# Raw weights of layer 1's first steps in four buffers, their mask on VectorE, and loads in another order

## The chip, the cores and the metric

One core of one Trainium2 chip runs the whole program. The metric is device microseconds of an execution, the median of several runs. TensorE (PE) does the matmuls, VectorE (DVE), ScalarE (ACT) and GpSimd (POOL) the elementwise work, and SyncE (SP) issues every DMA, in the order in which the program lists them. Each engine works through its own instructions in order; the engines wait for one another by semaphores.

## The reference

Three layers follow one another: random-feature attention over 32 heads (4 batches of 8, here 16 pairs of heads), and two feed-forward layers over 2304 tokens.

```python
def phi(x):                                   # q and k scaled by D**-0.25
    proj = np.einsum('bhsd,md->bhsm', x, omega)
    h = proj - np.sum(x * x, axis=-1, keepdims=True) / 2.0
    h = h - np.max(h, axis=-1, keepdims=True)
    return np.exp(h) / np.sqrt(m)
kv = np.einsum('bhsm,bhsd->bhmd', k_p, v)
num = np.einsum('bhsm,bhmd->bhsd', q_p, kv)
den = np.einsum('bhsm,bhm->bhs', q_p, np.sum(k_p, axis=2))[..., None] + 1e-06
x = num / den                                 # to (2304, 512)
h = x @ w_in;  x = (h - np.tanh(h)) @ w_out                      # layer 1
h = x @ w_in2; x = (h / (1.0 + np.exp(-1.702 * h))) @ w_out2     # layer 2
```

All is float32. The weights are 512 x 2048 and 2048 x 512.

## The kernel before, in words

**Attention** runs in 16 periods, k = 0 to 15, one per pair of heads (`period`, L420). A period multiplies q and k with omega (`att_a`, L106, and `att_b`, L134), sums keys with values (`att_c`, L161), multiplies the previous pair's queries with that (`att_d`, L178), and transposes the pair before (`att_e`, L202), whose result ScalarE rounds (`att_e_hi`, L216) and VectorE subtracts from (`att_e_lo`, L221). PSUM has four tiles `hs` and one each of `y0` to `y3`. `att_c` writes `y0`, which `att_a` also wrote and ScalarE copies out first (L113); `att_e` and `att_d` both write `y2` and `y3`. The last period has no `att_b`. What is left of attention after it (`tail0` to `tail2`) is put between the first three matmul steps of layer 1.

**The layers** run in two phases of eight weight slices each, over blocks of tokens in the orders of `ORDER` (L36): four blocks of 512 tokens and one of 256, whose number is 4. A step (the loop at L550, index `si`) takes one slice of one block of 512: h = x times w_in, 12 matmuls (`h_mm`, L299), and, three steps later, y += g times w_out, another 12 (`y_mm`, L346 in layer 1, L350 in layer 2). A block of 512 has eight steps, the block of 256 has four with two slices each. h(n) and y(n) below are those of step n. Twelve are needed because each float32 operand is split in two parts, hi and lo, and three of the four products are taken. The third of the twelve is the first to read a weight's lo part.

Between h and y stands `elem1` (L316) in layer 1: ScalarE takes the square s (L319), a second square (L320) and tanh (L321), rounds the previous step's result (`ghi`, L311) and writes the mask m (L323); VectorE does L324 and L326, POOL the product L325, then VectorE's copy_predicated (L327) takes the second branch where the mask is set. POOL subtracts `ghi` from the result (`glo`, L313), a step later and ahead of its product.

**Weights** come as raw 64-bit words and are rebuilt in `conv_mid` (L531): ScalarE's `conv1` (L247, L249) and VectorE's `conv2a` and `conv2b` (L253, L258) in one step, ScalarE's `conv3` (hi, L268) and POOL's `conv4` (lo, L272) a step later, behind the next half slice's `conv1` on ScalarE. A half slice is one unit, in the order of `US` (L41). Eight units are converted during attention. Units 8 to 15 are converted in steps 1 to 8, one each; h(4) to h(7) read units 8 to 11 and y(4) to y(7) read units 12 to 15. A raw unit lies in one of two buffers `raw`; its load (`load_w`, L234) is issued when `conv4` has freed the buffer of the unit two before.

**x blocks** lie in two buffers `xb`. The next block is loaded in four parts, one per step (L584 to L590); phases that begin with the block that the one before ended with share its buffer.

Of the kernel before, what the change touches and what calls it, by code (L numbers as in the profile page):

```python
# [11 lines left out]
I32 = mybir.dt.int32  # L12
I64 = mybir.dt.int64
U16 = mybir.dt.uint16
AF = mybir.ActivationFunctionType
ALU = mybir.AluOpType
# [7 lines left out]
FP = NF // 2  # L24
# [4 lines left out]
THR2 = 0.25 ** 2  # L29
# [10 lines left out]
NATT = 8  # L40
# [4 lines left out]
def body(ctx, tc, qT, kT, v, om, w1, w2, out):  # L45
    nc = tc.nc
    DRAM = bass.MemoryType.DRAM

    def pool(name, c=ctx, **k):
        return c.enter_context(tc.tile_pool(name=name, bufs=1, **k))  # L50
# [3 lines left out]
    cv = pool("conv")  # L54
# [5 lines left out]
    ap = pool("attn", early)  # L60
# [9 lines left out]
    tb = cp.tile([128, 1], F32, name="tb")  # L70
# [4 lines left out]
    def pt(tag):  # L75
        return ps.tile([128, 512], F32, tag=tag, name=tag, bufs=4 if tag == "hs" else 1)
# [4 lines left out]
    N16 = B * NP  # L81
# [6 lines left out]
    def load_k(i):  # L88
        if i < N16:
            kin[i] = ap.tile([128, S], F32, tag="kt", name="kt", bufs=2)  # L90
            nc.sync.dma_start(out=kin[i], in_=kT[i // NP, i % NP])
# [64 lines left out]
    def att_c(i):  # L156
        kp, vt = kps.pop(i), vin.pop(i)
        c = pt("y0")
        for j in range(2):
            for st in range(ST):  # L160
                nc.tensor.matmul(  # L161
                    c[:, j * DV:j * DV + DV], kp[:, j, st, :], vt[:, j, st, :], start=(st == 0), stop=(st == ST - 1))
        return c
# [66 lines left out]
    raws = {}  # L230
# [3 lines left out]
    def load_w(ci):  # L234
        if ci >= NU:
            return
        u = US[ci]
        i, part = divmod(u, 2)
        src = (w1, w2)[i // NF]
        raws[u] = cv.tile([128, 512, 2], I32, tag="raw", name="raw", bufs=2)  # L240
        nc.sync.dma_start(
            out=raws[u], in_=src[i % NF, :, part, :].bitcast(I32).rearrange("p (a b) -> p a b", b=2))


    def conv1(u):
        c = raws[u][:, :, 1].bitcast(F32)
        nc.scalar.activation(out=c, in_=c, func=AF.Copy, scale=2.0 ** -112)  # L247
        top = raws[u].bitcast(U16).rearrange("p a (b h) -> p a b h", h=2)[:, :, 0, 1]
        nc.scalar.activation(out=raws[u][:, :, 0], in_=top, func=AF.Copy, scale=0.9998 * 2.0 ** -13, bias=-0.4995)  # L249
# [27 lines left out]
    xblk = {}  # L277

    def new_x(key):
        xblk[key] = xp.tile([128, 2, ND, 512], F32R, tag="xb", name="xb", bufs=2)  # L280

    def load_x(key, part):
        src = (xs, ys)[key[0]]
        t0, n = BLOCKS[key[2]]
        if part == 0:
            new_x(key)
        hl, c = divmod(2 * part, ND)
        nc.sync.dma_start(
            out=xblk[key][:, hl, c:c + 2, :n].bitcast(F32),
            in_=src[hl, c:c + 2, :, t0:t0 + n].rearrange("c p t -> p c t"))  # L290
# [14 lines left out]
    def gtile(tag, bufs, dt=F32):  # L305
        return gp.tile([128, 512], dt, tag=tag, name=tag, bufs=bufs)
# [6 lines left out]
        nc.gpsimd.tensor_tensor(out=lo, in0=g, in1=hi.bitcast(F32), op=ALU.subtract)  # L313
        parts += [hi, lo]

    def elem1(h, us):  # L316
        s, t, w = gtile("s", 2), gtile("t", 2), gtile("wq", 2)
        m = gtile("m", 1, mybir.dt.bfloat16)
        nc.scalar.activation(out=s, in_=h, func=AF.Square)  # L319
        nc.scalar.activation(out=w, in_=s, func=AF.Square, scale=QS, bias=qb)  # L320
        nc.scalar.activation(out=t, in_=h, func=AF.Tanh)  # L321
        split_prev()
        nc.scalar.activation(out=m, in_=s, func=AF.Relu, bias=tb)  # L323
        nc.vector.scalar_tensor_tensor(out=w, in0=w, scalar=QC, in1=h, op0=ALU.add, op1=ALU.mult)  # L324
        nc.gpsimd.tensor_tensor(out=w, in0=w, in1=s, op=ALU.mult)  # L325
        nc.vector.tensor_tensor(out=t, in0=h, in1=t, op=ALU.subtract)  # L326
        nc.vector.copy_predicated(out=w, mask=m.bitcast(mybir.dt.uint16), data=t)  # L327
        conv_mid(us)
        return w

    def elem2(h, us):
        s = gtile("wq", 2)
        nc.scalar.activation(out=s, in_=h, func=AF.Sigmoid, scale=1.702)  # L333
        nc.vector.tensor_tensor(out=s, in0=h, in1=s, op=ALU.mult)  # L334
        split_prev()
        conv_mid(us)
        return s
# [56 lines left out]
        nc.sync.dma_start(out=ys[1, d, :, t0:t0 + n], in_=ye)  # L394


    oms = ap.tile([128, M], F32, name="oms")
    nc.sync.dma_start(out=oms, in_=om)
    load_k(0)
    load_q(0)  # L400
    load_k(1)
    load_v(0)
# [6 lines left out]
    def warm_up(n, tag):  # L409
        w = pt(tag)  # L410
        for i in range(n):
            nc.tensor.matmul(w, warm[:, :128], warm, start=True, stop=True)
# [4 lines left out]
    ci = [0]  # L417
    cprev, clast = [], []

    def period(k):  # L420
        old, new, last = cprev[:], [], clast[:]
        if 1 < k < 14 and k % 3:
            new.append(ci[0])
            ci[0] += 1
        cprev[:] = new
        clast[:] = old
        if k > 1:
            att_d_norm(k - 2, 1)
        if k > 0:
            att_sub(k - 1, 1)  # L430
            att_exp(k - 1, 1)
        for x in last:
            conv4(US[x], nc.vector)
        for x in old:
            conv2a(US[x])
        a = att_a(k)
        load_q(k + 2)
        if k + 1 < N16:
            tiles, mx = att_b(k + 1)
            load_k(k + 3)  # L440
        att_a_copy(k, a)
        if k == 0:
            make_identity(nc, ident)
            warm_up(1, "y3")
        if k > 1:
            parts = att_e_parts(k - 2, att_e(k - 2))
            att_e_hi(parts)
        if k + 1 < N16:
            for t in range(4):
                att_b_max(tiles, mx, t)  # L450
            for t in range(4):
                att_b_exp(k + 1, tiles, mx, t)
        if k > 1:
            att_e_lo(k - 2, parts)
        c = att_c(k)
        load_v(k + 2)
        att_c_copy(k, c)
        for x in old:
            conv2b(US[x])
        att_sub(k, 0)  # L460
        att_exp(k, 0)
        for x in old:
            conv3(US[x])
        if k == 1:
            load_w(0)
            load_w(1)
        for x in new:
            conv1(US[x])
        if k > 0:
            att_d(k - 1)  # L470
            att_d_norm(k - 1, 0)
        for x in last:
            load_w(x + 2)

    warm_up(2, "y0")
    tiles, mx = att_b(0)
# [5 lines left out]
    for k in range(N16):  # L482
        period(k)
# [20 lines left out]
    tails = [tail0, tail1, tail2]  # L504


    pend = deque()
    wnext = []
    steps = []
    seq = []  # L510
# [20 lines left out]
    def conv_mid(xs):  # L531
        for x in xs:
            conv1(US[x])
        for x in cprev:
            conv3(US[x])
            conv4(US[x], nc.gpsimd)
        for x in xs:
            conv2a(US[x])
            conv2b(US[x])
        wnext.extend(x + 2 for x in cprev)  # L540
        cprev[:] = xs

    def split_prev():
# [4 lines left out]
    gprev = []  # L548
    per = len(steps) // 4
    for si, (key, k, fs) in enumerate(steps):  # L550
        if si == len(tails):
            early.close()
            late["p"] = pool("late")
        moe, ph, bi = key
        n = BLOCKS[bi][1]
        ii = [moe * NF + f for f in fs]
        pos = seq.index(key)
        first, last = k == 0, fs[-1] == ph * FP + FP - 1
        h = h_mm(key, [wt[i] for i in ii], n)
        if si < len(tails):  # L560
            tails[si]()
        P, sp = divmod(si, per)
        us = []
        if P == 0 and sp <= 2 * FP - NATT:
            room = NATT - 2 * FP + sp
        else:
            room = min(2 * FP, max(0, (sp - (9 if P == 0 else 4)) * 2 * FP // 26))
        if ci[0] < 2 * FP * (P + 1) + room and conv_ok(ci[0]):
            us.append(ci[0])
            ci[0] += 1  # L570
        if first:
            y = [pt(f"y{d}") for d in range(ND if moe == 0 else n // 128)]
        ev = do_y() if len(pend) == LAG else None
        if ev:
            evac(*ev, 0)
        g = (elem2 if moe else elem1)(h, us)
        if ev:
            evac(*ev, 1)
        else:
            evac_split()  # L580
        gg = []
        gprev.append((g, gg))
        pend.append((key, y, ii, gg, first, last))
        xk = k - (1 if n == 512 else 0)  # L584
        if 0 <= xk < 4 and pos + 1 < len(seq):
            new = seq[pos + 1]
            if (new[0], new[2]) == (moe, bi):
                xblk[new] = xblk[key]
            else:
                load_x(new, xk)  # L590
        if ph and k >= FP // (512 // n) - 2:
            for d in range(2):
                load_part(moe, bi, d + 2 * (last))
        while wnext:
            load_w(wnext.pop(0))
    split(gprev.pop())
    while pend:
        ev = do_y()
# [43 lines left out]
```

## Time and profile before

| | us |
|---|---|
| median of 3 runs (942.77 to 944.05) | 943.16 |
| the profiled execution | 942.97 |
| its span | 941.2 |
| PE busy in it | 921.3 |
| DVE, ACT, POOL busy | 478.5, 515.7, 447.0 |

The span runs from the first to the last instruction; the execution's own time is 1.8 us more. TensorE is busy 98% of it, the other engines about half. A busy share of TensorE is not its speed: the profile also gives the clock that it was granted, in the mean 0.998 of the full one.

### The profile page before, as it was taken

The numbers are of one execution on the slowest core, as the hardware profiler recorded it, in microseconds if no ns is written. First come the engines' busy times: TensorE is split into PE (matmuls) and PEld (weight loads), VectorE is DVE, ScalarE is ACT, GpSimd is POOL, SyncE is SP. The second block draws the span as 40 slices with busy tenths as digits, with TensorE's granted clock in tenths as the row PEclk, the third lists the DMA queues.
The fourth block names the chain that finished last, engine by engine and source line by source line (L and its number), as shares of the span: only waits on it lengthen the run. The fifth ranks groups of instructions, "written<-read, shape, count | busy, mean of one in ns | idle before, by whom it ended". The sixth has DMA issues, their size and how long they took to land.

```text
span 941.2 us, 13426 instructions
## 1 busy us (share of the span) xinstructions
PE 921.3 (98%) x4918; PEld 775.5 (82%) x4918; DVE 478.5 (51%) x709; ACT 515.7 (55%) x1041; POOL 447.0 (47%) x330
## 2 busy tenths in 40 slices
PE   8999998899999999999999999999999999999998
PEld 6888886678888898888887888888888888888887
DVE  5999977566666653767767523432341212121212
ACT  6888867667768765777787624443442211211211
POOL 3555546555665653668686734433433222222221
PEclk9999999999999999999999999999999999999999
DMA  6777634252514243345464632425411233140302
GB/s 193 232 253 240 222 120 152 75 179 89 179 57 146 74 143 120 120 149 184 152 206 151 205 111 100 146 91 179 157 64 49 69 111 128 51 157 12 123 1 90
DMA packets 59890, 124.24 MB, mean 132 GB/s; under 512 B 6704, under 2 KB 11952, under 8 KB 59824
## 3 DMA queue, kind: packets, MB, share of 16 engines
q1 hardware_dynamic: 59824, 123.38, 39.5%
q8 instruction: 39, 0.64, 0.3%
q14 instruction: 27, 0.22, 0.1%
HBM read 90.32 MB, written 33.03 MB: 131 GB/s over the span
## 4 chain that ended last, share of the span: by engine, by line
PE 78%; POOL 6%; DVE 4%; ACT 4%; DMA 3%; issue 3%; SPq 1%; POOLq 0%; ACTq 0%; DVEq 0%
PE hs L299 34%; PE y L350 21%; PE y L346 14%; PE y L178 3%; PE y L161 3%; POOL wq L325 2%; DMA xb<-xs 2%; POOL glo L313 2%; POOL w L272 2%; PE y L106 1%; PE hs L134 1%; DVE wq L327 1%; DVE pq L120 1%; DMA raw<-w 1%; PE y L202 1%
## 5 line engine op out<-in xcount | busy, mean ns | idle before, releaser
L299 PE MATMUL hs<-xb,w 128*128 128x512 f32 (+1 forms) x1920 | 420.9, 369 | 5.8 <-POOL w L272 2.8
L299 PEld LDWEIGHTS hs<-xb,w 128*128 128x128 f32 x1920 | 335.3, 189 | 70.1 <-POOL w L272 4.5
L313 POOL TENSOR_TENSOR glo<-wq,ghi 128x512 fp32r<-128x512 f32 x144 | 192.2, 1335 | 392.2 <-ACT ghi L311 392.2
L346 PE MATMUL y<-ghi,w 128*128 128x512 f32 (+1 forms) x640 | 194.1, 371 | 4.2 <-ACT w L268 2.4
L333 ACT ACTIVATE wq<-hs 128x512 f32<-128x512 f32 x72 | 43.0, 597 | 271.9 <-PE hs L299 270.4
L350 PE MATMUL y<-w,ghi 128*128 128x512 f32 x576 | 188.6, 389 | 0.0
L334 DVE TENSOR_TENSOR wq<-hs,wq 128x512 f32<-128x512 f32 x72 | 49.6, 690 | 237.9 <-ACT wq L333 237.9
L327 DVE COPY_PREDICATED wq<-m,t 128x512 f32<-128x512 uint16 x72 | 99.3, 1379 | 117.2 <-POOL wq L325 115.1
L346 PEld LDWEIGHTS y<-ghi,w 128*128 128x128 f32 x640 | 116.9, 189 | 26.2 <-ACT w L268 2.9
L350 PEld LDWEIGHTS y<-w,ghi 128*128 128x128 f32 x576 | 108.2, 188 | 22.4
L346 PE MATMUL y<-glo,w 128*128 128x512 f32 (+1 forms) x320 | 118.2, 369 | 0.0
L350 PE MATMUL y<-w,glo 128*128 128x512 f32 x288 | 112.1, 389 | 0.0
L311 ACT CAST ghi<-wq 128x512 fp32r<-128x512 f32 x144 | 88.1, 612 | 25.7 <-DVE wq L327 24.9
L325 POOL TENSOR_TENSOR wq<-wq,s 128x512 f32<-128x512 f32 x72 | 93.1, 1292 | 15.1 <-DVE wq L324 15.1
L116 POOL PARTITION_ALL_REDUCE mq<-pq x32 | 64.4, 2059 | 63.7 <-ACT pq L114 60.0
L272 POOL TENSOR_TENSOR w<-raw,w 128x512 fp32r<-128x512 f32 x56 | 74.0, 1321 | 11.3 <-ACT w L268 11.3
L319 ACT ACTIVATE s<-hs 128x512 f32<-128x512 f32 x72 | 42.9, 596 | 64.5 <-PE hs L299 64.4
L346 PEld LDWEIGHTS y<-glo,w 128*128 128x128 f32 x320 | 60.6, 190 | 10.0
L350 PEld LDWEIGHTS y<-w,glo 128*128 128x128 f32 x288 | 54.1, 188 | 10.8
L258 DVE SCALAR_TENSOR_TENSOR raw<-raw 128x512 int32<-128x512 int32 x64 | 61.2, 957 | 1.9
L324 DVE SCALAR_TENSOR_TENSOR wq<-wq,hs 128x512 f32<-128x512 f32 x72 | 49.0, 680 | 18.6 <-ACT t L321 18.5
L320 ACT ACTIVATE wq<-s,qb 128x512 f32<-128x512 f32 x72 | 52.2, 725 | 6.6
(63 smaller groups left out, 927.7 us busy)
## 6 DMA issues: line engine op xcount, KB each, us to landing
raw<-w SPq DMA_DIRECT2D x64, 512.0 KB, 3.8
xb<-xs SPq DMA_DIRECT2D x28, 512.0 KB, 4.8
xb<-ys SPq DMA_DIRECT2D x28, 512.0 KB, 4.8
vt<-v SPq DMA_DIRECT2D x16, 325.0 KB, 3.3
kt<-kT SPq DMA_DIRECT2D x16, 288.0 KB, 3.2
qt<-qT SPq DMA_DIRECT2D x16, 288.0 KB, 3.1
op<-ye SPq DMA_DIRECT2D x18, 256.0 KB, 2.1
ye<-op SPq DMA_DIRECT2D x18, 256.0 KB, 6.1
```

The lines of the kernel that those rows point to most:

```text
L116: nc.gpsimd.partition_all_reduce(mqs[i, j], pq[:, j, :], channels=128, reduce_op=bass.bass_isa.ReduceOp.max)
L258: nc.vector.scalar_tensor_tensor(out=c, in0=c, scalar=3, in1=z, op0=ALU.logical_shift_left, op1=ALU.bitwise_or)
L272: eng.tensor_tensor(out=wt[i][:, part, 1, :], in0=raws.pop(u)[:, :, 1].bitcast(F32), in1=wt[i][:, part, 0, :].bitcast(F32), op=ALU.subtract)
L299: nc.tensor.matmul(h[:, j * n:j * n + n], w[:, 0, a, kt * 128:kt * 128 + 128], x[:, c, kt, :n], start=(k == 0), stop=(k == 11))
L311: nc.scalar.copy(out=hi, in_=g)
L313: nc.gpsimd.tensor_tensor(out=lo, in0=g, in1=hi.bitcast(F32), op=ALU.subtract)
L320: nc.scalar.activation(out=w, in_=s, func=AF.Square, scale=QS, bias=qb)
L325: nc.gpsimd.tensor_tensor(out=w, in0=w, in1=s, op=ALU.mult)
L327: nc.vector.copy_predicated(out=w, mask=m.bitcast(mybir.dt.uint16), data=t)
L334: nc.vector.tensor_tensor(out=s, in0=h, in1=s, op=ALU.mult)
L346: nc.tensor.matmul(y[d][:, :n], w[:, 1, a, d * 128:d * 128 + 128], g[c][:, j * n:j * n + n], **fl)
L350: nc.tensor.matmul(y[d], g[c][:, c0:c0 + 128], w[:, 1, a, :], **fl)
```

## The change

Units 8 to 15 get a tag of their own, `rw`, with four buffers in attention's pool, whose space is given back at step 9 instead of step 3. The first four of them are loaded in periods 12 to 15, the other four as `conv4` frees a buffer; `load_next` says what is loaded when a unit is done. Units 16 and 17 take the two `raw` buffers during attention. In steps 0 to 8 the mask is a comparison on VectorE (a tensor_scalar of s) instead of a Relu on ScalarE. A block's x may be loaded a block earlier where the phase in between shares its buffer, and in the block of 256 two parts per step, from its first step. The first key load is issued ahead of omega's; the zero matmul of period 0 is left out; in period 15 `att_c` stands ahead of `att_e`.

```diff
@@ load_w
-        raws[u] = cv.tile([128, 512, 2], I32, tag="raw", name="raw", bufs=2)
+        if NATT <= ci < 2 * FP:
+            raws[u] = ap.tile([128, 512, 2], I32, tag="rw", name="rw", bufs=4)
+        else:
+            raws[u] = cv.tile([128, 512, 2], I32, tag="raw", name="raw", bufs=2)
...
+    def load_next(ci):
+        if NATT <= ci < 2 * FP:
+            if ci + 4 < 2 * FP:
+                load_w(ci + 4)
+        else:
+            load_w(ci + 2 if ci >= 2 * FP or ci + 2 < NATT else ci + 2 + 2 * FP - NATT)
@@ elem1
-        nc.scalar.activation(out=m, in_=s, func=AF.Relu, bias=tb)
+        if si > 2 * FP - NATT:
+            nc.scalar.activation(out=m, in_=s, func=AF.Relu, bias=tb)
+        else:
+            nc.vector.tensor_scalar(out=m, in0=s, scalar1=THR2, scalar2=None, op0=ALU.is_gt)
@@ first loads
+    load_k(0)
     oms = ap.tile([128, M], F32, name="oms")
     nc.sync.dma_start(out=oms, in_=om)
-    load_k(0)
@@ period
             make_identity(nc, ident)
-            warm_up(1, "y3")
+        if k + 1 == N16:
+            c = att_c(k)
         if k > 1:
             parts = att_e_parts(k - 2, att_e(k - 2))
...
-        c = att_c(k)
+        if k + 1 < N16:
+            c = att_c(k)
...
         for x in last:
-            load_w(x + 2)
+            load_next(x)
+        if k > 11:
+            load_w(NATT + k - 12)
@@ conv_mid
-        wnext.extend(x + 2 for x in cprev)
+        wnext.extend(cprev)
@@ the steps
-        if si == len(tails):
+        if si == 2 * FP - NATT + 1:
             early.close()
...
-        xk = k - (1 if n == 512 else 0)
-        if 0 <= xk < 4 and pos + 1 < len(seq):
-            new = seq[pos + 1]
+        for new in seq[pos + 1:pos + 3]:
             if (new[0], new[2]) == (moe, bi):
                 xblk[new] = xblk[key]
-            else:
-                load_x(new, xk)
+                continue
+            if k == 0:
+                xnext[key] = deque(range(4)) if new not in xblk else deque()
+            for j in range(2 if n == 256 else 1):
+                if xnext[key] and (k > 0 or n == 256):
+                    load_x(new, xnext[key].popleft())
+            break
...
         while wnext:
-            load_w(wnext.pop(0))
+            load_next(wnext.pop(0))
```

In the orders below a row is line, operation, tile written <- tiles read, columns, and how many in a row. First TensorE's order in period 15 and up to h(1), before:

```order
L106 MATMUL y_1730<-qt,omd 128x64
L106 MATMUL hs<-qt,omd 128x64
L202 MATMUL y_1745<-ident,xt 128x128 x4
L202 MATMUL y_1746<-ident,xt 128x128
L161 MATMUL y_1760<-vt,kp 128x65 x10
L178 MATMUL y_1775<-kvz,pq 128x65 x6
L178 MATMUL y_1782<-kvz,pq 128x65 x4
L299 MATMUL hs<-xb,w 128x512 x12
L202 MATMUL y_1813<-ident,xt 128x128 x4
L202 MATMUL y_1814<-ident,xt 128x128
L299 MATMUL hs<-xb,w 128x512 x12
L178 MATMUL y_1857<-kvz,pq 128x65 x6
```

and after:

```order
L106 MATMUL y_1734<-qt,omd 128x64
L106 MATMUL hs<-qt,omd 128x64
L161 MATMUL y_1749<-vt,kp 128x65 x10
L202 MATMUL y_1760<-ident,xt 128x128 x4
L202 MATMUL y_1761<-ident,xt 128x128
L178 MATMUL y_1779<-kvz,pq 128x65 x6
L178 MATMUL y_1786<-kvz,pq 128x65 x4
L309 MATMUL hs<-xb,w 128x512 x12
L202 MATMUL y_1819<-ident,xt 128x128 x4
L202 MATMUL y_1820<-ident,xt 128x128
L309 MATMUL hs<-xb,w 128x512 x12
L178 MATMUL y_1863<-kvz,pq 128x65 x6
```

The ten matmuls of `att_c` (kp times vt) have moved ahead of the five transposes (ident and xt); `att_d` (kvz and pq) follows the transposes.

VectorE's order from the copy_predicated of one step to that of the next, between steps 3 and 4, before:

```order
L327 COPY_PREDICATED wq<-m,t 128x512
L253 SCALAR_TENSOR_TENSOR raw<-raw 128x512
L258 SCALAR_TENSOR_TENSOR raw<-raw 128x512
L324 SCALAR_TENSOR_TENSOR wq<-wq,hs 128x512
L326 TENSOR_TENSOR t<-hs,t 128x512
L327 COPY_PREDICATED wq<-m,t 128x512
```

and after:

```order
L340 COPY_PREDICATED wq<-m,t 128x512
L263 SCALAR_TENSOR_TENSOR rw<-rw 128x512
L268 SCALAR_TENSOR_TENSOR rw<-rw 128x512
L336 TENSOR_SCALAR m<-s 128x512
L337 SCALAR_TENSOR_TENSOR wq<-wq,hs 128x512
L339 TENSOR_TENSOR t<-hs,t 128x512
L340 COPY_PREDICATED wq<-m,t 128x512
```

The mask (m<-s) now stands between the second bit operation of the weight (rw or raw) and the first operation of the next step.

SP's order from the short block of phase 0 to that of phase 1 in layer 1 (raw are weights, xb parts of x, yp and ye partial y), before:

```order
L241 DMA raw<-w 128x1024 x4
L380 DMA yp<-ye 128x512 x4
L241 DMA raw<-w 128x1024
L288 DMA xb<-xs 128x2x512
L241 DMA raw<-w 128x1024
L288 DMA xb<-xs 128x2x512
L380 DMA yp<-ye 128x256 x4
L288 DMA xb<-xs 128x2x512
L362 DMA ye<-yp 128x256 x2
L288 DMA xb<-xs 128x2x512
L362 DMA ye<-yp 128x256 x2
```

and after:

```order
L244 DMA raw<-w 128x1024 x2
L298 DMA xb<-xs 128x2x512 x2
L244 DMA raw<-w 128x1024
L298 DMA xb<-xs 128x2x512 x2
L244 DMA raw<-w 128x1024
L393 DMA yp<-ye 128x512 x4
L244 DMA raw<-w 128x1024 x2
L393 DMA yp<-ye 128x256 x4
L375 DMA ye<-yp 128x256 x4
```

The four loads of x have moved ahead of the stores of the block before, and no load of x stands any more among the loads and stores of the short block's partial y.

## Rows read from the trace of the kernel before

**Rows 1.** TensorE's timeline, steps 4 to 9: start, us, what, [idle before]

```profile
148.54 2.60 PE L299 MATMUL hs<-xb,w 128*128 128x512 f32 x10 [0.84 <-POOL w L272]
...
174.30 0.50 PE L346 MATMUL y<-ghi,w 128*128 128x512 f32 x1 [2.42 <-ACT w L268]
...
175.68 0.74 PE L346 MATMUL y<-ghi,w 128*128 128x512 f32 x2 [0.65 <-POOL w L272]
...
189.00 0.74 PE L346 MATMUL y<-ghi,w 128*128 128x512 f32 x2 [0.51 <-POOL w L272]
```

**Rows 2.** List of waits: who for whom, us in all, times, longest

```profile
ACT raw L247 <- DMA raw<-w: 10.6, 6, 2.2
```

**Rows 3.** POOL's timeline in step 5: the weight subtraction

```profile
161.02 1.30 POOL L272 TENSOR_TENSOR w<-raw,w 128x512 fp32r<-128x512 f32 x1 [1.76 <-ACT w L268]
```

**Rows 4.** From the chain that ended last: start, us, what

```profile
175.68 3.97 PE y L346 x10
...
191.60 2.72 PE hs L299 x12
```

**Rows 5.** A stretch: busy us by engine, granted clock, DMA share, GB/s

```profile
178.00:180.00 2.00, 2.00 (x6) 1.51 (x6) 0.76 (x1) 0.70 (x2) 1.14 (x1) 0.52 0.25 98
```

**Rows 6.** TensorE's timeline at the two borders

```profile
356.87 2.15 PE L299 MATMUL hs<-xb,w 128*128 128x512 f32 x7
...
361.49 0.28 PE L346 MATMUL y<-ghi,w 128*128 128x256 f32 x1
...
643.82 1.75 PE L299 MATMUL hs<-xb,w 128*128 128x512 f32 x7
...
647.75 0.39 PE L350 MATMUL y<-w,ghi 128*128 128x512 f32 x1
```

**Rows 7.** Timelines of period 15 and tail0, TensorE and VectorE

```profile
123.38 0.77 PE L202 MATMUL y<-ident,xt 128*128 128x128 f32 x5
...
125.36 2.45 PE L161 MATMUL y<-vt,kp 128*128 128x65 f32 x20 [1.21 <-ACT pq L113]
...
127.64 2.40 PE L178 MATMUL y<-kvz,pq 128*128 128x65 f32 x20
...
132.66 0.71 PE L202 MATMUL y<-ident,xt 128*128 128x128 f32 x5
...
133.96 0.82 DVE L221 TENSOR_TENSOR xl<-y,xh 128x512 fp32r<-128x512 f32 x2 [2.39 <-ACT xh L216]
```

**Rows 8.** Groups by line: shapes, count, busy us, mean ns, idle before

```profile
L406 DVE TENSOR_SCALAR omd<-oms 128x128 f32<-128x128 f32 x1 | 0.2, 227 | 1.1 <-DMA oms<-om 1.1
...
L324 DVE SCALAR_TENSOR_TENSOR wq<-wq,hs 128x512 f32<-128x512 f32 x72 | 49.0, 680 | 18.6 <-ACT t L321 18.5
...
L190 DVE TENSOR_SCALAR rc<-y 128x6 f32<-128x6 f32 (+1 forms) x32 | 5.0, 155 | 0.0
```

**Rows 9.** Timelines of POOL and VectorE around 440 us

```profile
440.67 1.76 POOL L392 TENSOR_TENSOR ye<-ye,yh 128x512 fp32r<-128x512 f32 x1
...
439.47 1.85 DVE L327 COPY_PREDICATED wq<-m,t 128x512 f32<-128x512 uint16 x1 [1.25 <-POOL wq L325]
...
441.22 1.77 DVE L253 SCALAR_TENSOR_TENSOR raw<-raw 128x512 int32<-128x512 int32 x1
```

**Rows 10.** Timelines of VectorE and POOL in one undisturbed conversion step

```profile
479.52 1.84 DVE L327 COPY_PREDICATED wq<-m,t 128x512 f32<-128x512 uint16 x1 [2.50 <-POOL wq L325]
...
481.96 0.69 DVE L258 SCALAR_TENSOR_TENSOR raw<-raw 128x512 int32<-128x512 int32 x1
...
482.09 1.72 POOL L313 TENSOR_TENSOR glo<-wq,ghi 128x512 fp32r<-128x512 f32 x1 [1.35 <-ACT ghi L311]
...
485.09 1.84 DVE L327 COPY_PREDICATED wq<-m,t 128x512 f32<-128x512 uint16 x1 [1.24 <-POOL wq L325]
```

**Rows 11.** TensorE's timeline in period 1

```profile
14.20 0.69 PE L106 MATMUL y<-qt,omd 64*128 64x512 f32 x1 [0.63 <-ACT kvz L167]
```

**Rows 12.** DMA issues: KB each, median us to landing

```profile
raw<-w SPq DMA_DIRECT2D x64, 512.0 KB, 3.8
```

More of the change, by code (lines that the diff above doesn't have):

```diff
@@ L314, in split, with elem1 @@
         parts += [hi, lo]
-    def elem1(h, us):
+    def elem1(si, h, us):
         s, t, w = gtile("s", 2), gtile("t", 2), gtile("wq", 2)
@@ L507, in body @@
     pend = deque()
+    xnext = {}
     wnext = []
@@ L575, in body @@
             evac(*ev, 0)
-        g = (elem2 if moe else elem1)(h, us)
+        g = elem2(h, us) if moe else elem1(si, h, us)
         if ev:
```

## The prediction

> **What bounds the kernel now.** TensorE is busy nearly all the time, so I looked first for the places where it stands still, in the timeline of TensorE and in the list of waits; elsewhere it is fed without a gap and nothing that the change does can matter. There are two kinds of place.
>
> The first is layer 1's opening steps. In [rows 1] four of TensorE's waits stand with what ended them: the reader is to see that POOL's or ScalarE's write of a split weight releases TensorE, and that the third matmul of h(4) starts at 148.54 and that of y(4) at 175.68 us. Between them lie four steps of 6.79 us on average, where a step's 24 matmuls take 2 x 2.72 = 5.44 us [rows 4]. Why is the weight late? ScalarE waits for the raw weights six times, 10.6 us in all [rows 2]: a load starts when POOL's second half of an older weight has freed one of two buffers, and ScalarE cannot write the newer weight's first half before it, since that stands behind the waiting conversion. So POOL waits for ScalarE in turn (1.76 us at 161.02, [rows 3]), and load, conversion and subtraction form a ring that turns slower than TensorE. At 178 to 180 us the granted clock is 0.52, the 1.2 GHz level [rows 5], after TensorE had waited 2.42 and 0.65 us [rows 1]; ten matmuls then take 3.97 us where twelve take 2.72 at full clock [rows 4].
>
> The second kind is the block borders behind the 256-token block. [rows 6] shows h of the new block starting at 356.87 and the next y at 361.49: 4.62 us for work of 2.72, 1.90 lost. The other: 643.82 to 647.75, 1.21 lost. Both wait for the last part of x, issued in the short block's last step.
>
> **Borders: 3.1 us gained.** The parts of x are now issued a block earlier (first border) or two per step (second), at least two steps before they are needed, where they came in the step before. I take the whole 1.90 + 1.21 = 3.1 us. What could take it back is SP's order: loads of x now stand behind one raw load that waits for POOL, and the stores of partial y behind them; there are two steps for that. If the cover fails the gain is 0.
>
> **Order in the last attention period: 2.0 us lost.** Before, the transposes of head pair 13 run at 123.38, in the time in which TensorE waits 1.21 us for att_c's PSUM tile, and att_c follows at 125.36, att_d(14) at 127.64 [rows 7]. Att_c still waits for the same ScalarE copy; so it starts at 125.36 again, now with the gap empty, and the transposes come behind it, at 125.36 + (127.64 - 125.36) = 127.6. Att_d(14) writes the two PSUM tiles that the transposes wrote, so it also waits for ScalarE and VectorE to read them. How long that takes the next such pair shows: transposes at 132.66, VectorE's subtraction from 133.96, of which the first and larger of two takes 0.68 (as L324 does, [rows 8]): 1.98 us. Att_d(14) so starts at 129.6, 1.96 late, and TensorE runs from there to h(3) without waiting, so all that follows is late too. The bounds are 0 (if it is caught up behind) and 2.1 (both subtractions).
>
> **The mask on VectorE: 1.1 us more per step.** First its own time. A 128-column tensor_scalar takes 0.227 us (L406), a 512-column operation 0.680 (L324), a 6-column one 0.155 (L190) [rows 8]. The last two give 1.04 ns per column; at that pace 128 columns would take 0.28, so L406 runs at about half of it, and the mask takes 0.155 + 506 x 0.52 ns = 0.42 us. Bounds 0.23 and 0.68.
>
> Then where it stands. In VectorE's order it comes right behind the second bit operation of the weight conversion and ahead of the step's own L324. [rows 9] shows what can happen there: POOL's operation waits from 440.67 for VectorE's copy_predicated to end, and VectorE's next operation, L253, though ready, then takes 1.77 us, where L258, of the same kind, takes 0.69 undisturbed [rows 10]: the two engines exclude each other, and a waiting POOL goes ahead of VectorE's next. VectorE's operations with a PSUM operand (L324, [rows 8]) keep 0.68. Now one undisturbed conversion step [rows 10]: copy_predicated ends at 481.36 and, a step later, at 486.93, so a step takes 5.57 us; L258 begins at 481.96; POOL's L313 asks at 482.09, inside it, and ends at 483.81; then POOL's product, its weight subtraction and the next copy_predicated follow each other. The mask would stand behind L258 with L313 waiting: it starts at 483.81, takes 0.42, L324 0.68, and POOL's product starts at 484.9 instead of 483.8. The step becomes 5.57 + 1.1 = 6.67 us. This takes the mask for an operation that excludes POOL. Its operands are both in SBUF, as those of L253, L258 and L327 are, and none in PSUM, so those are the nearest rows; but they read two tensors and it reads one, so the other end (no exclusion, 5.57) stays as a rival.
>
> The Trainium skill speaks against the change here: "SBUF — State Buffer", section "Who interferes with whom", says that a tensor_scalar whose source and destination are in SBUF can run in a two-port mode, and that such an operation and a GpSimd instruction fully block each other; no row here shows it for that operation. By that page the step is the 6.67 us of the sum, without it 5.57.
>
> **Four raw buffers: the ring is gone, and the step of 6.67 takes its place.** The first eight weights' waits on DMA vanish; in their place stands the chain above. With h(4)'s third matmul at 148.54 + 1.96 + 1.1 = 151.6, y(4)'s comes four steps on, at 178.3, y(5)'s at 185.0, y(6)'s at 191.6. Step 9 has its mask on ScalarE again: y(7)'s at 197.2. Before, y(6) waits until 189.00 [rows 1], and y(7)'s third matmul comes 24 matmuls later, at 194.4. So steps 0 to 9 lose 2.8 us in all, the 1.96 among them. Between steps TensorE will wait over a microsecond each time, so a fallen clock is covered there, as is the relief of ScalarE, which had time to wait for DMA.
>
> **With one answer, nothing each.** The zero matmul in period 0: TensorE waits for ScalarE's kvz copy at 14.20 [rows 11] in any case, so its time is hidden. The key load ahead of omega: the first matmuls stand behind the two zero matmuls that remain. Four loads more in periods 12 to 15: a raw load takes 3.8 us to land [rows 12], no key or query load is left behind them that is needed sooner than one period later; one that came late would cost at most that.
>
> **Sum.** +2.8 - 3.1 = -0.3 us. Against the profiled execution (942.97 us, span 941.2) that is 942.7; against the median of the three runs, 943.16, it is 942.9, which I predict. A measurement tells about 0.2%, 1.9 us, from no change.
>
> **Rivals.**
> - The mask meets no POOL, or it is not held: the step stays 5.57, y(7) comes at 148.54 + 1.96 + 7 x 5.57 = 189.5, 4.9 early; with the borders 943.16 - 8.0 = 935.2. For it: a single source. Against: the pace of L406 looks like two columns at a time. 0.14.
> - The mask goes ahead of the waiting POOL: only its 0.42 is added, 6.0 a step; y(7) at 150.9 + 6 x 6.0 + 5.57 = 192.5, -1.9 - 3.1 = -5.0: 938.2. Against: rows 9. 0.08.
> - The late transposes cost nothing (slack in the steps behind): 942.9 - 2.0 = 940.9. 0.10.
> - Slower: the clock. In period 15 TensorE now waits 2.0 us ahead of att_c and 1.4 ahead of att_d. A fall like that at 176 costs 3.97 - 10 x 0.227 = 1.7 us, and there TensorE has no slack until h(3). One such stretch gives 944.6; held over both gaps, two: 946.3. It decides from the second on. Against: the 1.21 us before brought none. 0.12.
> - The borders keep their wait, because SP is held by raw loads: 942.9 + 3.1 = 946.0. 0.05.
> - The forecast: 0.48, from 941 to 945.2 with the mask between 0.23 and 0.68 us in six steps, the transposes and borders within 0.6. The last 0.03 is for what I don't see.
>
> Faster by over 0.2% (below 941.3): 0.14 + 0.08, most of the 0.10, and the forecast's low end, 0.35. Slower (above 945.0): most of the clock and border cases and the forecast's high end, 0.22. Within: 0.43. The range 937.5 to 946.3 leaves out the first rival and a little above.
>
> **What would show it.** In the profile after: no ScalarE wait on the raw load in steps 2 to 8; the mask's mean near 1.7 us rather than 0.42, behind L313; third matmuls of successive h 6.7 us apart; att_d(14) some 2 us later behind att_c; no TensorE wait at the two borders. A mask of 0.4 us with h steps of 5.6 would prove the first rival; a granted clock near 0.5 around 126 to 131 us the slower one.

## The result, and the profile after

The changed kernel takes 950.07 us (median of 6 executions, 948.69 to 955.95) beside 943.37 for the kernel before (6 executions): ratio 1.0076, 95% interval 1.005 to 1.0102. It is slower, and outside the predicted 937.5 to 946.3 us. The profiled execution takes 950.0 us, its span is 948.2 (941.2 before), its mean granted clock 0.987 (0.998 before).

I first laid TensorE's timelines of the two kernels beside each other at places that both have. These are rows of the one after (start, duration in us, line, operation, count, and in brackets the idle time ahead and what ended it):

```profile
124.97 0.69 PE L106 MATMUL y<-qt,omd 64*128 64x512 f32 x1
...
143.28 0.71 PE L202 MATMUL y<-ident,xt 128*128 128x128 f32 x5
...
160.41 2.57 PE L309 MATMUL hs<-xb,w 128*128 128x512 f32 x10 [1.37 <-POOL w L282]
...
167.04 2.56 PE L309 MATMUL hs<-xb,w 128*128 128x512 f32 x10 [0.89 <-POOL w L282]
...
186.87 0.73 PE L359 MATMUL y<-ghi,w 128*128 128x512 f32 x2 [2.92 <-POOL w L282]
...
200.23 0.73 PE L359 MATMUL y<-ghi,w 128*128 128x512 f32 x2 [0.56 <-POOL w L282]
...
368.10 2.91 PE L309 MATMUL hs<-xb,w 128*128 128x512 f32 x12
370.85 0.28 PE L359 MATMUL y<-ghi,w 128*128 128x256 f32 x1
...
652.50 2.88 PE L309 MATMUL hs<-xb,w 128*128 128x512 f32 x12
...
657.94 2.88 PE L309 MATMUL hs<-xb,w 128*128 128x512 f32 x12
```

| place | before | after | late by |
|---|---|---|---|
| att_a(15) | 122.15 | 124.97 | 2.82 |
| transposes ahead of h(1) [rows 7] | 132.66 | 143.28 | 10.62 |
| third matmul of y(4) [rows 1] | 175.68 | 186.87 | 11.19 |
| third matmul of y(6) [rows 1] | 189.00 | 200.23 | 11.23 |
| first border, h [rows 6] | 356.87 | 368.10 | 11.23 |
| and the y behind it [rows 6] | 361.49 | 370.85 | 9.36 |
| second border, h [rows 6] | 643.82 | 652.50 | 8.68 |
| and the next h | 650.48 | 657.94 | 7.46 |
| span | 941.2 | 948.2 | 7.0 |

The table is the account: 2.82 us are lost up to the last attention period, 7.80 in it and in h(0), 0.61 in steps 1 to 6, and then 1.87, 0.67 and 1.22 are won (the middle one between the borders, where before a y waited 0.63 us for VectorE at 509.70), and 0.46 behind TensorE's last matmul, which is still 7.46 late; no run here explains that end. The steps and the borders did about what was forecast. What was not in the sum lies in the first 143 us.

**The first loss** stands at the start. The matmul of [rows 11] now reads:

```profile
11.17 2.45 PE L161 MATMUL y<-vt,kp 128*128 128x65 f32 x20 [1.44 <-ACT pq L113]
14.64 1.22 PE L106 MATMUL y<-qt,omd 64*128 64x512 f32 x1 [1.03 <-ACT kvz L167]
```

It starts 0.44 us later than in [rows 11] and takes 1.22 us instead of 0.69. The windows say why (from:to, length, then busy time of PE, PEld, DVE, ACT, POOL with counts, the granted clock as a share of 2.4 GHz, DMA share, GB/s):

```profile
12.00:14.00 2.00, 1.61 (x15) 1.47 (x14) 0.77 (x2) 2.00 (x10) 2.00 (x2) 0.89 0.09 33
14.00:16.00 2.00, 1.36 (x4) 0.84 (x6) 1.76 (x2) 1.27 (x4) 1.93 (x3) 0.50 0.57 164
...
18.00:20.00 2.00, 2.00 (x16) 1.78 (x14) 1.12 (x2) 0.69 (x4) 0.38 (x1) 0.50 0.61 150
20.00:22.00 2.00, 2.00 (x18) 2.00 (x18) 0.95 (x4) 2.00 (x10) 2.00 (x2) 0.90 0.56 153
```

Where the second zero matmul stood TensorE now idles 1.44 us, and behind that the clock is at 1.2 GHz: by the shares of the windows from about 13.6 to 20.4 us. Before it was 1.00 in all of them. Of the 2.82 us, 2.82 - 0.44 = 2.4 are lost behind that matmul's start.

**The second loss** is period 15, which [rows 7] showed of before:

```profile
128.18 3.25 PE L161 MATMUL y<-vt,kp 128*128 128x65 f32 x20 [1.91 <-ACT pq L113]
131.22 1.27 PE L202 MATMUL y<-ident,xt 128*128 128x128 f32 x5
133.73 4.53 PE L178 MATMUL y<-kvz,pq 128*128 128x65 f32 x20 [1.23 <-DVE xl L221]
138.01 5.43 PE L309 MATMUL hs<-xb,w 128*128 128x512 f32 x12
```

```profile
128.00:130.00 2.00, 1.82 (x15) 1.82 (x15) 0.00 (x0) 0.84 (x4) 1.67 (x1) 0.91 0.00 0
130.00:132.00 2.00, 2.00 (x11) 2.00 (x11) 0.00 (x0) 0.00 (x0) 2.00 (x2) 0.50 0.00 0
...
140.00:142.00 2.00, 2.00 (x7) 1.52 (x5) 0.00 (x0) 0.57 (x1) 0.00 (x0) 0.50 0.00 0
142.00:144.00 2.00, 2.00 (x10) 1.60 (x9) 0.00 (x0) 0.04 (x1) 0.00 (x0) 0.68 0.00 0
```

By the same shares the clock is at 1.2 GHz from about 129.6 to 143.3 us. All that TensorE does between is drawn out: the transposes 1.27 instead of 0.77, att_d(14) 4.53 instead of 2.40 [rows 7]. Counted from att_a(15), att_c(15) starts 3.21 us later in both kernels; att_d(14) starts 3.27 us later than before, and from its start to that of h(0), and from there to the transposes, another 2.08 and 2.45 are lost: 7.80 in all.

**The mask** did what the sum said. It takes 0.42 us where POOL is idle, and 1.53 where POOL's `glo` has asked first, at 161.69 (the rows of VectorE and POOL):

```profile
145.32 0.42 DVE L336 TENSOR_SCALAR m<-s 128x512 bf16<-128x512 f32 x1
...
162.17 1.53 DVE L336 TENSOR_SCALAR m<-s 128x512 bf16<-128x512 f32 x1
163.62 0.68 DVE L337 SCALAR_TENSOR_TENSOR wq<-wq,hs 128x512 f32<-128x512 f32 x1
...
161.69 1.72 POOL L323 TENSOR_TENSOR glo<-wq,ghi 128x512 fp32r<-128x512 f32 x1 [1.33 <-ACT ghi L321]
```

The third matmuls of h(4) and h(5) are 167.04 - 160.41 = 6.63 us apart (6.67 forecast). Of ScalarE's waits on raw weights [rows 2] one of 0.72 us is left, at 447.09 and so outside these steps.

### The profile page after: what moved, and what is told of

The parts are those of the page before. It is cut to its first block, busy times and chain, and to the rows that moved or that the text cites. A ratio compares the mean times of both kernels' runs of the same rounds, so it can differ in the third digit from the quotient of the medians.

```text
span 948.2 us, 13415 instructions
## 1 busy us (share of the span) xinstructions
PE 927.8 (98%) x4916; PEld 782.9 (83%) x4916; DVE 485.6 (51%) x718; ACT 510.7 (54%) x1032; POOL 450.0 (47%) x330
## 4 chain that ended last, share of the span: by engine, by line
PE 80%; DVE 2%; issue 2%; POOL 1%; ACT 1%; POOLq 0%; ACTq 0%
PE hs L309 40%; PE y L363 21%; PE y L359 20%; POOL wq L338 1%; DVE m L336 1%; PE y L178 0%; DVE wq L337 0%; DVE rw L263 0%; DVE rw L268 0%; POOL w L282 0%; DVE wq L340 0%; DVE xl L221 0%; ACT wq L330 0%; ACT xh L216 0%; ACT s L329 0%
## 5 line engine op out<-in xcount | busy, mean ns | idle before, releaser
L323 POOL TENSOR_TENSOR glo<-wq,ghi 128x512 fp32r<-128x512 f32 x144 | 194.5, 1351 | 389.5 <-ACT ghi L321 389.5
L340 DVE COPY_PREDICATED wq<-m,t 128x512 f32<-128x512 uint16 x72 | 103.5, 1437 | 113.6 <-POOL wq L338 111.5
L282 POOL TENSOR_TENSOR w<-raw,w 128x512 fp32r<-128x512 f32 x48 | 64.3, 1339 | 2.3 <-ACT w L278 2.2
L268 DVE SCALAR_TENSOR_TENSOR raw<-raw 128x512 int32<-128x512 int32 x56 | 50.5, 902 | 1.7
```

The source lines that it names most:

```text
L268: nc.vector.scalar_tensor_tensor(out=c, in0=c, scalar=3, in1=z, op0=ALU.logical_shift_left, op1=ALU.bitwise_or)
L282: eng.tensor_tensor(out=wt[i][:, part, 1, :], in0=raws.pop(u)[:, :, 1].bitcast(F32), in1=wt[i][:, part, 0, :].bitcast(F32), op=ALU.subtract)
```

## The experiments

My theory after this reading was that the two lost stretches are the clock's, and that the mask holds the steps. The rivals were that the waits, the order of loads, or the four buffers are what costs. In what follows a time is the median of a kernel's executions. Executions of one kernel differ, and the longer ones mostly have a lower mean granted clock; where that matters it stands beside the time. The experiments ran in three groups, each on a chip of its own and beside the kernel before: 943.82 us beside `c_back`, `zero_back`, `both_back` and `gap_filled`, 944.39 beside `both_back_act`, `act_filled`, `border` and `mask_alone`, 943.69 beside the others. A difference across groups carries what lies between these.

**One part undone.** `c_back` puts att_c(15) back behind att_e(13):

```diff
-        if k + 1 == N16:
-            c = att_c(k)
         if k > 1:
             parts = att_e_parts(k - 2, att_e(k - 2))
...
-        if k + 1 < N16:
-            c = att_c(k)
+        c = att_c(k)
```

> The changed kernel with one part undone: att_c(15) stands behind att_e(13) again. Theory 'clock': in the changed kernel PE waits 1.91 us before att_c(15), the granted clock falls to 0.50 from about 130 to 142 us, and of the 7.8 us that period 15 and h(0) lose 2.0 are the wait and 5.8 the clock. Then here the clock reads 1.00 in all windows of 124 to 140 us, h(1) starts some 7.8 us sooner than in the changed kernel (at about 136 us instead of 143.75), and the time is 942.3 us (941 to 944). Theory 'wait only': the clock falls here too, 2.0 us are won, 948 us. Theory 'the loss is the mask and the buffers, in the steps': what is won at h(1) is waited for again in steps 1 to 9, 949 to 950 us.

Measured: 946.58 us, single executions from 940.92 (clock 0.996) to 950.92 (0.987). That lies between the two: the two shortest executions, 940.92 and 941.69, are near what the first theory forecast, and in the profiled one (span 945.2) the clock falls in period 15 all the same, as the second had it, behind a wait of only 1.22 us:

```profile
128.16 3.23 PE L161 MATMUL y<-vt,kp 128*128 128x65 f32 x20 [1.22 <-ACT pq L113]
131.19 4.47 PE L178 MATMUL y<-kvz,pq 128*128 128x65 f32 x20
135.42 5.06 PE L309 MATMUL hs<-xb,w 128*128 128x512 f32 x12
```

So the new order is not needed for the fall. `zero_back` puts the zero matmul back and keeps the new order:

```diff
         if k == 0:
             make_identity(nc, ident)
+            warm_up(1, "y3")
```

> The changed kernel with one part undone: the second zero matmul stands again in period 0, behind make_identity. Theory 'clock at the start': without it PE idles from 10.0 to 11.2 us, and the clock is at 0.50 from 13.8 to 20.3 us, which costs 2.4 us; the key load ahead of omega costs the other 0.4. Then here the clock reads 1.00 from 12 to 22 us, att_a(15) starts at 122.6 us (124.97 in the changed kernel, 122.15 before) and the time is 947.7 us, the fall in period 15 being still there. Rival 'load order': the zero matmul is worth nothing and the key load costs all 2.8; att_a(15) at 125, 950 us. A second rival: PE is 2.4 us ahead of the other engines at period 15 and waits longer there, 949 us or more.

Measured: 948.02 us. In its profile the clock is 1.00 from 8 to 24 us and att_a(15) starts at 122.84: the start is mended, as the first theory said. In period 15 the clock falls in that execution; by the mean clocks not in all, since they run from 943.2 (clock 0.996) to 948.89 (0.991).

`both_back` is the two edits together:

> The changed kernel with both undone: the second zero matmul is back and att_c(15) stands behind att_e(13). Left of the change are the four buffers, the mask on VectorE, the loads at the borders, and the key load ahead of omega. Theory 'clock': 2.4 and 7.8 us come back, 939.9 us (938.5 to 942), the clock reads 1.00 everywhere but around 185 us, where the steps wait. Rival 'the steps are the limit': POOL's products 6.62 us apart give a part back as a longer wait of y(4) (2.92 us in the changed kernel), 942 to 944 us.

Measured: 941.65 us, ratio to before 0.9971 (0.9959 to 0.9982), executions from 940.77 to 943.21. Of the 10.2 us expected 8.4 came back: inside the first theory's 938.5 to 942, 0.35 under the rival's. What did not come back lies in the steps, as the rival had it. From the transposes ahead of h(1) to the third matmul of y(6) are 56.34 us before, 56.95 in the changed kernel and 59.10 here. By h(4) 1.1 us of that have gathered (h(3) waits 1.46 us for VectorE's L339, 0.57 in the changed kernel); another 1.0 lies between y(4) and y(6), 14.38 us apart here and 13.36 there. By the shares of windows of 1 us the clock is low for 6.8 us here, from 176.0, within y(4)'s wait, to 182.8, and in the changed kernel for 3.4 behind that wait, from 187.6 to 191.1:

```profile
177.23 1.22 PE L359 MATMUL y<-ghi,w 128*128 128x512 f32 x2 [2.91 <-POOL w L282]
191.61 0.73 PE L359 MATMUL y<-ghi,w 128*128 128x512 f32 x2 [0.56 <-POOL w L282]
```

Period 15 runs at full clock behind the same 1.22 us wait that `c_back` has:

```profile
125.17 2.45 PE L161 MATMUL y<-vt,kp 128*128 128x65 f32 x20 [1.22 <-ACT pq L113]
127.45 2.40 PE L178 MATMUL y<-kvz,pq 128*128 128x65 f32 x20
129.65 3.02 PE L309 MATMUL hs<-xb,w 128*128 128x512 f32 x12
```

**The clock alone.** `gap_filled` keeps the changed kernel's order and its waits, and only gives TensorE something to do in them; the added products are read by nothing:

```diff
         if k + 1 == N16:
+            warm_up(2, "y3")
             c = att_c(k)
...
+        if k + 1 == N16:
+            warm_up(1, "y1")
         if k > 0:
             att_d(k - 1)
```

> The changed kernel with its own order kept (att_c(15) ahead of att_e(13)) and three matmuls of zeros added that nothing reads: two ahead of att_c(15), into the y3 tile, and one between att_e(13) and att_d(14), into the y1 tile. They fill PE's waits of 1.91 and 1.23 us and take no wait away. Theory 'clock': it reads 1.00 from 128 to 142 us, att_c, the transposes, att_d(14) and h(0) take 2.45, 0.77, 2.40 and 2.98 us again instead of 3.25, 1.27, 4.53 and 5.43, h(1) starts 5.5 us sooner, and the time is 944.5 us (943.5 to 946.5). Rival 'the order costs by its waits': the waits are what they were, the added matmuls cost up to 1 us on top, 950 to 951 us.

Measured: 944.24 us, 5.8 less than the changed kernel, all ten executions within 943.31 to 945.35. TensorE does more work and the program is shorter:

```profile
126.12 1.96 PE L425 MATMUL y<-warm 128*128 128x512 f32 x4
127.94 2.45 PE L161 MATMUL y<-vt,kp 128*128 128x65 f32 x20
130.22 0.71 PE L202 MATMUL y<-ident,xt 128*128 128x128 f32 x5
130.78 1.02 PE L425 MATMUL y<-warm 128*128 128x512 f32 x2
132.27 2.45 PE L178 MATMUL y<-kvz,pq 128*128 128x65 f32 x20 [0.47 <-DVE xl L221]
134.53 3.02 PE L309 MATMUL hs<-xb,w 128*128 128x512 f32 x12
137.38 0.71 PE L202 MATMUL y<-ident,xt 128*128 128x128 f32 x5
```

From att_a(15), here at 124.73, to the transposes ahead of h(1) are 12.65 us; before they were 132.66 - 122.15 = 10.51, in the changed kernel 143.28 - 124.97 = 18.31. So 5.7 of the 7.8 us of period 15 are the clock, and 2.1 the waits with the added matmuls in them.

`c_back_filled` does the same to `c_back`, with one zero matmul in the 1.2 us gap:

```diff
+        if k + 1 == N16:
+            warm_up(1, "hs")
         c = att_c(k)
```

> As c_back (no second zero matmul, att_c(15) behind att_e(13)), and one matmul of zeros in the 1.2 us gap ahead of att_c(15). c_back spread from 940.9 to 950.9 us; its profiled execution has the clock at 0.50 both at 14 to 20 us and at 130 to 138 us. Theory 'the spread is the clock in that gap': here the clock reads 1.00 from 124 to 140 us, what is left is the start, 2.4 to 2.8 us over both_back's 941.65: 944.4 us, with no execution over 946. Rival 'the clock falls anyway, from what happened at the start': 946.6 us and the same spread.

Measured: 943.39 us instead of 946.58, no execution over 945.25. In the profile att_c(15) waits 0.35 us instead of 1.22 and the clock stays at 1.00 (windows as above):

```profile
126.00:128.00 2.00, 1.65 (x10) 0.82 (x8) 0.74 (x2) 1.76 (x6) 0.40 (x1) 1.00 0.00 0
128.00:130.00 2.00, 2.00 (x20) 2.00 (x19) 1.23 (x3) 0.78 (x4) 2.00 (x2) 1.00 0.22 85
```

So most of the 10 us over which `c_back` spread came from that gap; 4.7 are left. The start is still low here, at 0.50 from 14 to 18 us. One execution, 940.6 us, has a mean clock of 1.00: the start does not fall every time either.

**Why there and not in `both_back`?** Two kernels shift `both_back` with more zeros ahead of everything (`shift_2` has three, `shift_4` four):

```diff
-    warm_up(2, "y0")
+    warm_up(4, "y0")
```

> As both_back, with three zero matmuls at the start instead of two: everything behind comes some 1.9 us later, at full clock. both_back's clock never fell in period 15 (spread 2.4 us), c_back's fell in most executions, with the same 1.22 us wait 3 us later. Theory 'the fall at the start carries over': no start fall, so no fall in period 15, 943.5 us with a spread of 2 to 3 us. Rival 'it is where the wait stands in time': the clock falls at 130 us in many executions, 947 to 949 us or a wide spread.

> As shift_2 with four zero matmuls at the start: some 3.8 us later than both_back, about where c_back stands. Theory 'the fall at the start carries over': 945.4 us, spread 2 to 3 us. Rival 'where the wait stands in time': the clock falls in period 15 in many executions, 949 to 951 us, or a spread of 5 us and more.

Measured: 944.18 us and 946.63, where `both_back` has 941.65. The shift was smaller than I took it for: att_a(15) starts at 122.64 and 123.42, 0.7 and 1.5 us behind `both_back`. In both profiled executions the clock is 1.00 at the start and falls in period 15; of `shift_4`:

```profile
14.00:16.00 2.00, 1.37 (x12) 0.99 (x13) 1.73 (x1) 1.39 (x6) 2.00 (x2) 1.00 0.13 18
126.00:128.00 2.00, 1.37 (x11) 1.37 (x11) 0.18 (x1) 1.90 (x7) 1.22 (x1) 0.92 0.00 0
128.00:130.00 2.00, 2.00 (x11) 2.00 (x11) 1.85 (x3) 0.00 (x0) 2.00 (x2) 0.50 0.64 241
```

A fall at the start is not needed, so the theory that it carries over is out. The same instructions with the same 1.22 us wait fall where they begin 0.7 to 1.5 us later. The rival's price was 2 to 5 us too high, and `shift_2`, from 943.4 (clock 0.996) to 945.3 (0.993), seems to fall only in some executions.

But the place in time does not settle it either. Here are att_c(15) of `shift_2`, of `both_back_act` (the next experiment, up to there the same program as `both_back`) and of `shift_4`:

```profile
125.85 2.73 PE L161 MATMUL y<-vt,kp 128*128 128x65 f32 x20 [1.22 <-ACT pq L113]
126.06 2.45 PE L161 MATMUL y<-vt,kp 128*128 128x65 f32 x20 [1.22 <-ACT pq L113]
126.63 3.61 PE L161 MATMUL y<-vt,kp 128*128 128x65 f32 x20 [1.22 <-ACT pq L113]
```

The middle one stands between the two that fall and keeps 1.00. The two shifts were also taken in another group than `both_back`, and `both_back` was not run again there. What decides the fall stays open.

**The mask and the buffers.** `both_back_act` is `both_back` with the mask on ScalarE in all steps:

```diff
-        if si > 2 * FP - NATT:
-            nc.scalar.activation(out=m, in_=s, func=AF.Relu, bias=tb)
-        else:
-            nc.vector.tensor_scalar(out=m, in0=s, scalar1=THR2, scalar2=None, op0=ALU.is_gt)
+        nc.scalar.activation(out=m, in_=s, func=AF.Relu, bias=tb)
```

> As both_back, and the mask on ScalarE in all steps. Left of the change are the four buffers, the loads at the borders and the key load ahead of omega. Theory 'the mask made the new chain': without the mask in VectorE's way POOL's products lose their 6.62 us spacing and come every 5.6 to 5.8 us (ScalarE's work of a step), y(4)'s wait of 2.91 us and the low clock at 176 to 183 us go, y(6)'s wait comes at 183 to 185 us instead of 191.61, and the time is 934 us (931 to 937), some 7 us under both_back. Rival 'POOL's own work is the chain': its product, ghi-glo difference and raw part need 6.6 us a step without the mask too, the spacing stays, 941 us. Rival 'ScalarE takes the mask back and is the chain': 6.2 us a step, 938 us.

Measured: 934.81 us, ratio to before 0.989 (0.9863 to 0.9917). It beats both kernels. POOL's weight subtractions come every 5.6 us (rows of POOL):

```profile
154.73 1.30 POOL L282 TENSOR_TENSOR w<-rw,w 128x512 fp32r<-128x512 f32 x1
160.30 1.33 POOL L282 TENSOR_TENSOR w<-rw,w 128x512 fp32r<-128x512 f32 x1
165.92 1.31 POOL L282 TENSOR_TENSOR w<-rw,w 128x512 fp32r<-128x512 f32 x1
```

and the long wait of y(4), 2.92 us in the changed kernel, is 1.26, with the clock at 1.00 behind it:

```profile
172.82 0.73 PE L356 MATMUL y<-ghi,w 128*128 128x512 f32 x2 [1.26 <-POOL w L282]
184.56 0.72 PE L356 MATMUL y<-ghi,w 128*128 128x512 f32 x2 [0.44 <-POOL w L282]
```

So the mask on VectorE costs 941.65 - 934.81 = 6.8 us where the four buffers have taken the ring away, or 7.4 by what each gains on the kernel before in its own group (2.2 and 9.6). The longer low clock of `both_back` behind y(4) is in that. `mask_alone` is the kernel before with only that mask:

> The kernel before with the mask on VectorE in the first steps alone. Theory: the ring of two raw buffers spaces the steps at 6.79 us, the mask's chain needs 6.62, so the steps keep their spacing and the time is that of before, 943.4 us (943 to 945). Rival 'the two add up': the mask's 1.1 us comes on top of the ring, since the raw buffer is freed by work that stands behind the mask on VectorE and POOL: up to 7.7 us a step over 8 steps, 950 us.

Measured: 946.59 us, ratio 1.0022 (1.0006 to 1.0038): 2.2 us more than before in its group, with 0.6 to 3.6 in the interval, between the two forecasts. From h(4) to y(4) its steps are 6.88 us on average, near the ring's 6.79; most of what it adds comes at the ends, where h(4)'s third matmul starts at 150.16 instead of 148.54 [rows 1] and those of y(4) and y(6) are 13.99 us apart instead of 13.32.

`border` is the kernel before with the loads at the borders alone:

> The kernel before with the loads at the borders alone. By the two waits of before, 1.90 and 1.21 us, 3.1 us are won: 940.3 us. Rival 'more is won': between step 10 and the end the changed kernel came back by 4.4 us, which would be the waits and some 0.6 us at 509 us and 0.7 elsewhere: 939.0 us. Rival 'the earlier loads collide with others': 942 us or no change.

Measured: 940.36 us, ratio 0.9958 (0.994 to 0.9977). No wait of TensorE on a load of x is left in its list. The median is the one forecast; the medians' difference in that group, 944.39 - 940.36 = 4.0, would fit the rival, and the interval doesn't separate 3.1 from 3.8.

**The small ones again, on the better kernel.** `no_zero_act` is `both_back_act` without the second zero matmul:

> As both_back_act without the second zero matmul: what that one matmul is worth where the mask is on ScalarE. Theory: the clock is at 0.50 from 14 to 20 us, 2.4 to 2.8 us: 937.4 us, and up to 5 us more in executions whose clock falls in period 15 too: 937 to 942, wide spread. Rival 'what is lost at the start is waited for anyway in the steps': 935 us.

Measured: 940.34 us, 5.5 more for one matmul of zeros less (across two groups; the kernel before differs by 0.7 between them the other way); single executions from 935.7 (clock 0.996) to 941.04 (0.991). The profiled one falls twice, at the start and in period 15:

```profile
16.00:18.00 2.00, 2.00 (x18) 1.49 (x16) 0.31 (x1) 1.25 (x3) 0.46 (x1) 0.50 0.01 3
...
136.00:138.00 2.00, 2.00 (x6) 1.52 (x6) 1.30 (x4) 0.54 (x1) 0.00 (x0) 0.50 0.05 20
```

`act_filled` is `both_back_act` with the added line of `c_back_filled`:

> As both_back_act, with one matmul of zeros more that nothing reads, in period 15 between att_e(13) and att_c(15), where PE waits 1.2 us for ScalarE's copy. Theory 'the clock falls in that gap in some executions': c_back and the kernel before spread over 5 to 10 us between executions, with the mean clock lower in the slow ones; here the median stays within 0.5 us of both_back_act and no execution lies over 2 us above the lowest. Rival 'the gap doesn't matter there': the spread is that of both_back_act, and the median rises by up to 0.5 us, since the added matmul ends after the copy.

Measured: 935.45 us, 934.22 to 935.96. There was no fall to prevent in `both_back_act` (933.7 to 935.65), so this tells nothing on the theory. The filler costs nothing that shows in the trace: from att_a(15) to att_c(15) are 3.21 us in both kernels. The medians, of four executions each, are 0.6 us apart.

## Why the prediction was wrong, point by point

- **Nothing for the zero matmul: wrong, and the first step that failed.** The step looked at when TensorE's next wait ends [rows 11], and that is ScalarE's copy in either case. It did not ask what the idle time does to the matmuls behind. They ran at 1.2 GHz, and a kernel is 2.1 us (the changed one beside `zero_back`), 4.9 us (`c_back` beside `both_back`) and 5.5 us (`no_zero_act` beside `both_back_act`) slower without it. Of that 2.1 to 2.4 us are the start; in the two larger ones the clock, by its means, also falls in period 15 in most executions of the kernel without it, and not in `both_back` and `both_back_act`. Why the one goes with the other stays open with the question above.
- **2.0 us for the order in period 15: the wait was right, the term was not.** From 131.22 to 133.73 the transposes and the two engines behind them take 2.51 us at half clock, 1.98 forecast at full; with the clock held (`gap_filled`) period 15 loses 2.1, about what was forecast. The clock stood among the rivals, at 0.12 and 1.7 us a stretch. That price came from ten matmuls [rows 4, 5]; here the low clock lasted over part of att_c, the transposes, att_d and h(0), and cost 7.80 - 1.96 = 5.8 (5.7 by `gap_filled`). So the mechanism stood in the list and its price was the failed term: 3.4 us for both gaps, where 5.8 came. The argument against it, that the 1.21 us wait of before brought no fall, rested on one execution. `c_back` and `shift_4` fall behind a wait as long.
- **"A fallen clock is covered" in the steps: only in part.** Around y(4) the clock is low for 3.4 us in the changed kernel as before, and y(6) follows y(4) by 13.36 us (13.32 before). In `both_back` it is low for 6.8 us and y(6) follows by 14.38 (in `shift_2` 6.8 and 14.47): that 1.0 us is not covered. And what is late ahead of h(1) is not made up at all: 10.62 us there, 11.23 at y(6).
- **The mask: right.** 0.42 us alone, held behind POOL, steps of 6.63 instead of 6.67 us. The two rivals on it are out. The Trainium skill ("SBUF — State Buffer", section "Who interferes with whom") says that a tensor_scalar can enter a two-port mode, and that such an operation and a GpSimd instruction then block each other, whichever issues first going ahead; the trace agrees, with 1.53 us behind POOL beside 0.42.
- **Steps 0 to 9: right in the changed kernel.** At y(6) 191.6 - 189.00 - 1.96 = 0.64 us were forecast beyond the order, and 0.61 are measured (0.34 in `gap_filled`). It holds less well than that looks: in `both_back`, with h(3)'s longer wait and the longer low clock, the same steps lose 2.76. What the sum did not say is what `both_back_act` shows: with the mask left on ScalarE the four buffers (and the key load) win another 940.36 - 934.81 = 5.5 us over `border`, which the mask took back.
- **The borders: right.** 3.1 us forecast, 1.87 + 1.22 = 3.09 measured. The 0.67 us more in the account are a wait for VectorE at 509.70. It is gone in `mask_alone` too, which keeps the old loads, and back in `both_back_act` (0.66 us), so it is not the borders' doing; what sets it is not shown.
- **The key load ahead of omega: no cost shown.** With it, att_c(0) starts at 11.17 us in one execution and at 10.71 in another (`c_back_filled`), before at 11.23; my expectation for `zero_back` had put 0.4 us on it.

Forecast +2.8 - 3.1; measured 2.82 + 7.80 + 0.61 - 3.76 - 0.46 = 7.0 us. The two stretches of low clock are 2.4 and 5.8 of it.

## What to carry to other kernels

A matmul that computes nothing may be holding the clock: before it is taken out, or before work is moved out of a gap of TensorE, cost the matmuls behind the gap at half clock, all of them until the granted clock is back, not only the gap. A wait of 1.2 us behind which the clock holds in one profile is no proof, since in another execution, or a microsecond earlier or later, it can fall behind the same wait; where a gap can't be closed, a filler that nothing reads cost little here. When one resource is relieved (the ring of loads) and another engine is loaded in the same edit (the mask), measure them apart: here the mask took 6.8 us where the buffers gave 5.5.

## What the runs showed of the hardware that I had not expected

- The granted clock falls to 0.50 behind gaps of 1.2 to 1.9 us among the matmuls of attention, though not behind each of them, and stays there for 6.8 us (start) to 13.7 us (period 15), though TensorE works through most of that.
- Whether it falls behind a given gap changes between executions. The kernel before seems to do it too: of the 31 executions beside the first group of experiments the fastest took 942.26 us at a mean clock of 0.998, the slowest 946.66 at 0.994. The Trainium skill ("TensorE: Matmul & The Clock Gate", Part 1) says that the clock's monitor runs free of the kernel's start. The spread of one kernel agrees with that (`c_back`, 940.92 us to 950.92), and so does `both_back_act`, which holds its clock between the places where `shift_2` and `shift_4` lose it. It does not by itself explain that all five executions of `shift_4` have a mean clock of 0.992 or 0.993 and all ten of `both_back` 0.996 to 1.000, and no run here shows the monitor itself.
